# Attention scores in narrower pieces, a new order for the first 620 tasks, and a last projection by tiles

## The chip, the core and the metric

The kernel runs on one core of one Trainium2 chip. The metric is the time of one execution on the device in microseconds; each time below is from the chip. The engines are named as the profile names them: PE is TensorE's matmul, PEld its weight load, DVE VectorE, ACT ScalarE, POOL GpSimd, and SP the engine whose queue issues every DMA of this kernel.

## What is computed

Two layers follow each other. The first is attention over q, k and v of shape (4, 8, 768, 64), that is 4 batches, 8 heads, 768 positions of 64 numbers. A query sees two kinds of keys: its neighbours at a distance under 16, and one summary per block of 32 positions, whose key is the maximum over the block and whose value is the mean:

```python
k_sum = k.reshape(B, H, nb, block, D).max(axis=3)
v_sum = v.reshape(B, H, nb, block, D).mean(axis=3)
scores_l = scale * np.matmul(q, k.transpose(0, 1, 3, 2))
mask_l = np.abs(pos[:, None] - pos[None, :]) < window
scores_s = scale * np.einsum('bhsd,bhnd->bhsn', q, k_sum) + np.log(block)
scores_all = np.concatenate([np.where(mask_l, scores_l, -1e9), scores_s], axis=-1)
a = softmax(scores_all)
attn_out = np.matmul(a, np.concatenate([v, v_sum], axis=2))
```

The second layer takes the 3072 rows of 512 numbers, projects them to 2048, applies softplus and projects back: `out = softplus(x @ w_in) @ w_out`.

## The kernel before, in words

**Units of work.** The 768 queries of a batch are cut into chunks of 256; two chunks make a group, so there are six groups x = 0 to 5 of 512 rows. The attention of one chunk and one pair of head pairs (a head pair is two heads on the 64 + 64 partitions) is a block of tasks in `attention` (line 614): scores on PE, mask on DVE (line 657: adds the mask, takes the row minimum of the negated scores), exp on ACT (line 665), inverse on DVE, normalize on POOL, DVE or ACT (line 678 or 681), transposes of the probabilities (for group 0 by PE at line 698 and a copy by ACT at line 702; else by DVE at line 711 and a trip through DRAM), values on PE (line 744, for group 0 also 752), and copies of the result (line 765; 784 and 788 for a rounded high part by ACT and a low part by DVE).

**Scores.** A window is 64 queries with their 96 possible local keys; after those come 24 block summaries, 120 columns in all. In groups 2 to 5 the 120 columns are copied together and one matmul per window and head takes them all. In groups 0 and 1 ("apart") they lie apart: `scores` (line 629) first does the windows, 64 queries by 96 keys each (line 637), and then, per 128 queries and head, the 24 summaries in a second matmul (line 644). Each scores task of that kind covers two head pairs (`NG` = 2). The operands are plain fp32, and each such matmul stands as two records in the trace. There are eight such tasks. All scores share one PSUM tile, `sc`, which is free again when the mask has read it.

**Feed-forward.** `feed_forward` (line 1134) goes over 16 slices f of the hidden dimension. A product (line 1057, tile `ph`; in the later half line 1097, tiles `hx` and `hy`, by a scheme that saves one product in eight) is followed by softplus twice on ACT: "rounded" (line 1159, tile `gh`) and "exact" (line 1163). Their difference is the "rest" (line 1167, DVE, tile `gl`). Then `project` (line 1170) multiplies gh and gl with the two parts of w_out into four PSUM tiles `po`, one per 128 rows, accumulating over f. For f of the first and last slice there is a task per tile; between, all four tiles together. Each group goes through the slices in two halves, whose first result (`part`) is kept in DRAM. At the end, line 1197 reloads it, DVE adds it (line 1204), and the result is stored; for group 0, which comes last, one store per 128 rows (line 1225).

**Weights** arrive in pairs of slices, w0 to w7, and are split into a rounded part and a low part by a row of steps: magnitude (931 on DVE or 934 on ACT), clamp (938), shift (942), sign (946) on DVE, tail (952 on ACT or 955 on DVE), add_tail (960, POOL), high (964, ACT or DVE), low (971, DVE or POOL).

**What sets the order.** Every task has a number, in the order in which the program text declares it. `SEQUENCE` (line 147) lists all of them in the order in which they are issued; each engine works its own tasks in that order, and a task that waits holds back what is behind it on its engine. A letter behind a number picks another engine for a task: 54 is POOL's normalize, 54b ACT's. SP's queue is ordered by the same list.

Numbers that the text below uses: 3 to 22 are twenty warming matmuls on the identity (line 1249); 23, 25, 27, 29 load the keys of the first batch and 24, 26, 28, 30 take their maxima (line 352, DVE); 31 to 41, odd, load values whose sums PE forms in 32 to 42, even (line 430), and 43 is their mean (line 441, ACT); 44 and 47 load q of the first block, 82 and 85 that of the next head pairs, and 45 to 49 and 83 to 87 the value windows; 50, 66, 88, 104 are the scores of group 0 and 291, 316, 358, 383 those of group 1; 51, 67, 89, 105 the masks; 97 is the values task of chunk 0, second half of the heads; 120 to 123 ("keep", line 447) copy the first mean into its place; 125 and 134 load the two halves of the first slices of w_in, 161 the whole second pair; 218 is the first product of the feed-forward and 222 its rest.

Of the kernel before, what the change touches and what calls it, by code (L numbers as in the profile page):

```python
# [147 lines left out]
23 124 0 125 2 3 25 4 44 47 5 134 161 6 7 24 8 31 27 9 10 126 130 35 11 127 12 128 13 129 14 26 131 33 50 1 132 133a  # L148
51 15 16 52 17 85 18 135 136 66 19 137 20 138 29 21 22 45 82 162 139 37 163 166 53 32 164 54b 165 39 41 67 167 34 284
48 143 68 36 28 55 30 140 57 88 46 168 69 38 49 89 70 40 56 58 90 104 86 180 169 42 84 141a 105 142a 43 106 291 91 59  # L150
309 148a 92a 144 145 146 83 87 147 152 107 170 71 61 108 171 63 62 73 72 292 74 75 334 338 293 149 64 60a 181 93 182
95 183 316 77 79 184 94 96 97 351 76 80 150a 185 120 199 78 294 295a 153a 109 157 154 111 155 110 156 112 113 296 317
158 101 99 100 176 102 151a 159 218 336 115 117 160a 318 297 342 340 116 227 346 98a 118 186 285 121 335 219 339 228
172 173 174 220 319 358 221 229 222 230 223 376 289 337a 114 320b 234 235 224 175 344 286 204 231 177 298 301 299 290
321 241 343 236 287 300 242 187 237 178 341a 225 243 244 226 179 232 288 322 345 359 189 360 233 123 122 239 190 238
245 347 200a 188 302 310 361 383 201 362b 323 348 314 202 240 248 203 468b 472a 205 363 312 313 249 246 303 469b 467
384 326 324 191a 385 325 315 311 255 195a 206a 192 207 364 208 209 256 193 386 194 247 250 251 257 475 252 196 258 327
494b 259 387b 498a 262 349a 365 368 366 263 352 355 328 350 493 356 197a 269 388 367 198a 210a 270 476 353 357 354 495
253 264 211 389 65 643 265 212 214 213 254 271 266 501 272 215 273 369 519 477 260 377 380 216a 217 378 381 261 520a
478 526 521b 390 393 267 370 307 479a 305 308a 306a 372 392 391 382 480 268 373a 329 379 274 502 481 641 278 645 503  # L160
276 330a 332a 333a 277 275 529 394 547 331 548a 549 374a 375 395 399 482 485 484 470 279 397a 398 400 401 402 504 473
483 103 471 474 505 410 403 404 554a 281 282 405 644 506 411 406 412 413 530 507 407 649 647 408 414 409 531 557 486
659a 660b 417 532 533a 418 534 508 509 415 419 648 558 487a 420 510 511 496 500 658 653 304 497 416 421 499 559 655
535 422 642 650 646 665 651 652 424 560 425 561a 426 668 686 427 428 512 513 522 525 536 81 431 438 432 423 429 430
562 669 524 539 537 527 654 517 670 518a 489a 687 693a 523 528 538 563 439 433 440 434 435 441 442 688b 436 671 672b
696 715a 714 119 540 541a 491a 545 550 556 564 566 543a 492a 490a 673 697 719 716 567 552 565 445 446 447 448 437 443
449 656 553 551 555 698 444 396 371 674 450 544 722 741a 742a 699 700a 568 452 569 675 661 573 574 453 515 571a 280
572a 701 546a 516a 575 454 455 283 663 740 745a 576 451 577 578 456 458 488 723 457 459 678 676 657 460 461a 584 585
# [63 lines left out]
def kernel(  # L232
# [243 lines left out]
    class Places:  # L476


        def __init__(self, c, hp, sums, pads, apart):
# [11 lines left out]
            if apart:  # L491
                self.k_keys = [key for g in range(NG) for key in (sums.key_of(hp + g), (sums.k, hp + g))]
                self.keys = [[lambda g=g, s=s: sums.keys(hp + g)[:, s:s + KW] for s in starts] for g in range(NG)]
                self.k_sums = lambda g: sums.k()[:, hp + g]
            else:
                self.k_keys = [(k, "sums")]
                self.keys = [[lambda g=g, w=w: k()[:, g, w] for w in range(NWIN)] for g in range(NG)]
# [47 lines left out]
    class FirstPlaces:  # L545


        def __init__(self, hp, sums, own, sp):
# [29 lines left out]
            for i in range(n_c):  # L578
                w0 = i * NWIN
                tiles = SimpleNamespace(apart=True, q_keys=q_keys, v_keys=v_keys, k_keys=k_keys)  # L580
                tiles.q = lambda g, i=i: q(g)[:, i * CH:(i + 1) * CH]
                tiles.v = lambda g, w0=w0: v(g)[:, w0:w0 + NWIN]
                tiles.sums = lambda g: sums.first(hp + g)
                c0 = i * NG * NU * KS
                tiles.sp = lambda c0=c0: sp()[:, c0:c0 + NG * NU * KS].rearrange("p (u k) -> p u k", k=KS)
                tiles.sp_key = (sp, i)
                tiles.keys = [
                    [lambda g=g, s=s: sums.keys(hp + g)[:, s:s + KW] for s in starts[w0:w0 + NWIN]] for g in range(NG)
                ]
                tiles.k_sums = lambda g: sums.k()[:, hp + g]  # L590
                self.tiles.append(tiles)
# [22 lines left out]
    def attention(x, i, hp, tiles, by_pe):  # L614
# [518 lines left out]

    def feed_forward(x, f0, f1):
        po = [buffer([P, DM], F32, "po", "po", NT, psum) for _ in range(NT)]
        pairs = f0 > 0
        for f in range(f0, f1):
# [32 lines left out]
            def project(tokens, which, f=f, w2=w2, i2=i2, gh=gh, gl=gl):  # L1170
                for t in tokens:
                    for i, (a, part) in enumerate(((gh, 0), (gh, 1), (gl, 0))):
                        if (a is gl) in which:
                            nc.tensor.matmul(  # L1174
                                po[t](), lhsT=a()[:, t * P:(t + 1) * P], rhs=w2()[:, part, i2 * DM:(i2 + 1) * DM],
                                start=f == f0 and i == 0, stop=f == f1 - 1 and i == 2,
                            )
            parts = [(w2, i) for i in range(2)]
            if f in (f0, f1 - 1):
# [9 lines left out]
        order.group = f"e{x}.{f1}"  # L1189
        for i in range(0, NT, 2):  # L1190
# [28 lines left out]
            elif x == 0:  # L1219

                for t in range(2):
                    r0 = groups[x][0] * CH + (i + t) * P

                    def leave(t=t, r0=r0, ob=ob):
                        nc.sync.dma_start(out=out[r0:r0 + P, :], in_=ob()[:, t])
                    order.add(SP, 0, leave, [(ob, t)], [], size=256 * KiB, row=2048)
# [121 lines left out]
```

## Time and profile before

| | us |
|---|---|
| median of three runs | 616.25 |
| lowest and highest | 616.2 and 620.01 |
| the profiled execution | 617.61 |
| its span, first to last instruction | 615.8 |
| PE busy | 607.9 |
| DVE busy | 381.2 |
| ACT busy | 343.6 |
| POOL busy | 180.2 |

The profiled execution is one run by itself; its time is 1.8 us more than its span. Busy times come from the trace; matmuls are pipelined, so neighbouring records overlap.

### The profile page before, as it was taken

To read this page: it belongs to the slowest core of one execution; us is meant where nothing else is said; L and a number is where in the kernel's file an instruction comes from. 1 tells how busy PE (TensorE), PEld (TensorE's weight loads), DVE (VectorE), ACT (ScalarE), POOL (GpSimd) and SP (SyncE) were. 2 spreads that over 40 slices of the span, in tenths; PEclk is the share of its full clock that TensorE was granted. 3 is DMA by queue.
4 is the path that set the end of the run, shared out by engine and by line. 5 is a ranking of instruction groups with operands and counts; after the bars stand their busy time and mean duration, and the time that the engine had idled before them with its cause. 6 is when DMAs were issued, how large, how long until landed. Compare 5 with 4: busy or idle time off the path is not lost.

```text
span 615.8 us, 11948 instructions
## 1 busy us (share of the span) xinstructions
PE 607.9 (99%) x4444; PEld 509.2 (83%) x4444; DVE 381.2 (62%) x990; ACT 343.6 (56%) x846; POOL 180.2 (29%) x178
## 2 busy tenths in 40 slices
PE   8999999999999999999999999999999999999997
PEld 6577878888888888888888888889898989999996
DVE  4799997866565765533335679854765664554532
ACT  3889898977768675665356986432313222132211
POOL 4415334324115032210002563572410315012000
PEclk8999999999999999999999999999999999999999
DMA  8978679866868666666427620031040230020121
GB/s 303 304 253 256 213 244 281 265 218 200 277 203 259 203 214 205 209 205 212 134 69 237 238 74 1 1 141 64 2 171 2 102 137 1 35 103 1 40 98 68
DMA packets 66569, 96.12 MB, mean 156 GB/s; under 512 B 5872, under 2 KB 44624, under 8 KB 65744
## 3 DMA queue, kind: packets, MB, share of 16 engines
q1 hardware_dynamic: 66512, 95.36, 47.6%
q8 instruction: 35, 0.57, 0.4%
q14 instruction: 22, 0.18, 0.1%
HBM read 66.06 MB, written 27.26 MB: 152 GB/s over the span
## 4 chain that ended last, share of the span: by engine, by line
PE 88%; ACT 5%; DVE 2%; DMA 2%; issue 1%; POOL 1%; SPq 0%; ACTq 0%
PE po L1174 39%; PE ph L1057 21%; PE hx L1097 9%; PE hy L1097 7%; PE xo L744 4%; PE sc L637 4%; PE sc L644 1%; DMA first<-qT_dram 1%; DMA part<-ob 1%; PE vt L430 1%; PE warm L1249 1%; ACT t L934 1%; ACT L934 1%; ACT L1159 1%; ACT raw L952 1%
## 5 line engine op out<-in xcount | busy, mean ns | idle before, releaser
L1174 PE MATMUL po<-w,gh 128*128 128x512 f32 x768 | 202.8, 392 | 0.4 <-DVE w L971 0.4
L1174 PEld LDWEIGHTS po<-w,gh 128*128 128x128 f32 x768 | 141.3, 188 | 29.9 <-DVE w L971 0.8
L1057 PE MATMUL ph<-xw,w 128*128 128x512 f32 x672 | 161.5, 391 | 0.0
L1057 PEld LDWEIGHTS ph<-xw,w 128*128 128x128 f32 x672 | 125.2, 188 | 27.4 <-issue 0.5
L1174 PE MATMUL po<-w,gl 128*128 128x512 f32 x384 | 114.3, 392 | 0.0
L1174 PEld LDWEIGHTS po<-w,gl 128*128 128x128 f32 x384 | 70.9, 188 | 14.6 <-issue 0.3
L665 ACT ACTIVATE sp<-sp,nm 128x120 f32<-128x120 f32 x192 | 73.1, 383 | 7.1 <-DVE nm L657 6.9
L1159 ACT ACTIVATE gh<-hx 128x512 fp32r<-128x512 f32 x20 | 12.0, 599 | 107.6 <-DVE hx L1107 107.6
L960 POOL TENSOR_TENSOR t<-t,raw 128x1024 int32<-128x1024 int32 (+1 forms) x20 | 40.7, 2041 | 105.6 <-DVE t L946 70.7
L1167 DVE TENSOR_TENSOR gl<-ph,gh 128x512 fp32r<-128x512 f32 x56 | 38.2, 687 | 51.2 <-ACT ph L1163 51.0
L1159 ACT ACTIVATE gh<-ph 128x512 fp32r<-128x512 f32 x56 | 33.3, 597 | 37.6 <-PE ph L1057 37.3
L801 POOL TENSOR_TENSOR x<-r,x 128x512 fp32r<-128x512 f32 x23 | 30.6, 1339 | 67.9 <-DVE x L794 58.2
L657 DVE CUSTOM_DVE_ANT_0 sp<-sc,added 128x120 f32<-128x120 f32 x192 | 40.8, 278 | 8.6 <-PE sc L644 2.8
L665 ACT ACTIVATION_READ_ACCUMULATOR sp<-sp,nm 128x1 f32 x192 | 36.0, 188 | 0.0
L1097 PE MATMUL hx<-x,w 128*128 128x256 f32 x240 | 35.7, 285 | 0.0
L1097 PE MATMUL hx<-x,sw 128*128 128x256 f32 x240 | 35.5, 284 | 0.0
L1097 PEld LDWEIGHTS hx<-x,w 128*128 128x128 f32 x240 | 32.9, 190 | 2.1
L1097 PE MATMUL hy<-x,sw 128*128 128x256 f32 x240 | 34.4, 284 | 0.0
L1159 ACT ACT_TABLE_LOAD x23 | 29.5, 1283 | 6.3 <-PE ph L1057 5.9
L1163 ACT ACTIVATE ph<-ph 128x512 f32<-128x512 f32 x56 | 32.8, 590 | 0.0
L1097 PEld LDWEIGHTS hx<-x,sw 128*128 128x128 f32 x240 | 32.0, 190 | 0.8
L1097 PEld LDWEIGHTS hy<-x,sw 128*128 128x128 f32 x240 | 31.2, 192 | 0.2
(116 smaller groups left out, 821.8 us busy)
## 6 DMA issues: line engine op xcount, KB each, us to landing
squares<-tb SPq DMA_DIRECT2D x20, 512.0 KB
pT<-squares SPq DMA_DIRECT2D x80, 128.0 KB
raw<-w_out_dram SPq DMA_DIRECT2D x16, 512.0 KB
kf<-kT_dram SPq DMA_DIRECT2D x16, 384.0 KB
raw<-w_in_dram SPq DMA_DIRECT2D x6, 1024.0 KB
q<-qT_dram SPq DMA_DIRECT2D x20, 256.0 KB
raw<-r SPq DMA_DIRECT2D x20, 256.0 KB
part<-ob SPq DMA_DIRECT2D x10, 512.0 KB
```

The source lines that it names most:

```text
L637: nc.tensor.matmul(unit(g * NU + h * NPAIR + i)[r * QW:(r + 1) * QW, :KW if tiles.apart else KS], lhsT=q[rows, w * QW:(w + 1) * QW], rhs=t ...
L657: nc.vector.tensor_tensor_reduce(out=sp()[:, n], in0=unit(n), in1=added()[:, kinds.index((lows[w], lows[w + 1]))], scale=-SCALE, scalar=FL ...
L665: nc.scalar.activation(sp()[:, n], sp()[:, n], AF.Exp, bias=nm()[:, n:n + 1], scale=-1.0, accum_out=ss()[:, n:n + 1],)
L744: nc.tensor.matmul(xo()[h * D:(h + 1) * D, g * CH + w * QW:g * CH + (w + 1) * QW], lhsT=v[:, h * D:(h + 1) * D], rhs=queries(g, w, h)[:KW ...
L801: engine.tensor_tensor(to(1), a(), to(0).bitcast(F32), op=ALU.subtract)
L960: nc.gpsimd.tensor_tensor(a, a, word(0, I32), op=ALU.add)
L1057: nc.tensor.matmul(ph(), lhsT=lhs(part, cc), rhs=xw[cc][0]()[:, xw[cc][1], a], start=cc == 0 and n == 0, stop=cc == NCC - 1 and n == 2,)
L1097: nc.tensor.matmul(to()[:, half], lhsT=lhs(wa, cc), rhs=of_x(xa)[:, cc * CH:(cc + 1) * CH], start=cc == 0 and m == 0, stop=cc == NG - 1 an ...
L1159: nc.scalar.activation(gh(), all_of(), AF.Softplus)
L1163: nc.scalar.activation(all_of(), all_of(), AF.Softplus)
L1167: nc.vector.tensor_sub(out=gl(), in0=all_of(), in1=gh().bitcast(F32))
L1174: nc.tensor.matmul(po[t](), lhsT=a()[:, t * P:(t + 1) * P], rhs=w2()[:, part, i2 * DM:(i2 + 1) * DM], start=f == f0 and i == 0, stop=f == ...
```

## The change

It has three parts.

1. In `scores`, the apart kind handles the 24 summaries per window of 64 queries, right behind the window's own matmul and with the same queries as weights, where before it did them per 128 queries behind all windows. The lists `keys` now give pieces (first column, end column, key tile), and `k_sums` is gone.

```diff
-                            nc.tensor.matmul(
-                                unit(g * NU + h * NPAIR + i)[r * QW:(r + 1) * QW, :KW if tiles.apart else KS],
-                                lhsT=q[rows, w * QW:(w + 1) * QW], rhs=tiles.keys[g][w]()[rows], start=True, stop=True,
-                            )
-                for i in range(NPAIR if tiles.apart else 0):
-                    for h in range(2):
-                        rows = slice(h * D, (h + 1) * D)
-                        nc.tensor.matmul(
-                            unit(g * NU + h * NPAIR + i)[:, KW:KS],
-                            lhsT=q[rows, i * P:(i + 1) * P], rhs=tiles.k_sums(g)[rows], start=True, stop=True,
-                        )
+                            for k0, k1, k in tiles.keys[g][w]():
+                                nc.tensor.matmul(
+                                    unit(g * NU + h * NPAIR + i)[r * QW:(r + 1) * QW, k0:k1],
+                                    lhsT=q[rows, w * QW:(w + 1) * QW], rhs=k[rows], start=True, stop=True,
+                                )
```

2. The first 620 entries of `SEQUENCE` are put in another order. They hold the same tasks; the letter, and so the engine, of some fifty of them changes. Its beginning:

```diff
-23 124 0 125 2 3 25 4 44 47 5 134 161 6 7 24 8 31 27 9 10 126 130 35 11 127 12 128 13 129 14 26 131 33 50 1 132 133a
-51 15 16 52 17 85 18 135 136 66 19 137 20 138 29 21 22 45 82 162 139 37 163 166 53 32 164 54b 165 39 41 67 167 34 284
+44 0 47 3 23 4 25 2 5 125 161 6 31 27 7 33 85 8 9 10 11 24 12 13 14 26 15 50 82 130 126 127 128 29 16 129 17 134 18 51
+1 131 52 19 20 35 66 21 162 22 163 37 166 164 28 45 53 49 165 54b 32 34 48 67 167 39 68 55 30 132a 88 133 135 41 139a
...
```

Up to task 222, these change their engine: 132 and 139 (a high part and a tail, 512 wide) go from ACT to DVE; 133 and 142 (low parts, 512 wide) and 70 and 108 (normalize) from POOL to DVE; 60 (a copy of 512) and 150 (a high part) from DVE to ACT; 98 and 114 (copies) swap DVE and ACT. On SP, 120 and 121 move ahead of the value loads 86, 84 and 87.

3. The last two slices of the last group are projected tile by tile in a new function, `finish`: for each of the four tiles, the three matmuls of either slice, the addition, and the store. In the last tile, the first slice is added on its own; the second slice goes in halves of 256 columns to the PSUM tile of the scores, and each half is added and stored alone.

```diff
+        for t in range(NT - 1):
+            ob = (obs[t // 2], t % 2)
+            order.add(PE, 0.7, lambda t=t: p0([t], every), in0, [po[t]])
+            order.add(PE, 0.7, lambda t=t: p1([t], every), in1, [po[t]])
+            total(t, po[t], 0, DM, ob)
+            leave(t, 0, DM, ob)
+        t = NT - 1
+        whole = (obs[t // 2], t % 2)
+        order.add(PE, 0.7, lambda: p0([t], every), in0, [po[t]])
+        total(t, po[t], 0, DM, whole)
+        for k in range(2):
+            c0, c1, key = k * half, (k + 1) * half, (*whole, k)
...
+            order.add(PE, 0.36, lambda at=bank_of, c0=c0, c1=c1: p1([t], every, to=at, c0=c0, c1=c1), in1, [(other, k)])
+            total(t, (other, k), c0, c1, key, bank_of)
+            leave(t, c0, c1, key)
```

`total` is the addition of line 1204 over the given columns, `leave` the store of line 1225. The reloads stay where they were in the sequence.

## Rows read from the trace of the kernel before

**Rows 1.** The page: busy us, share of the span, instructions, per engine

```profile
PE 607.9 (99%) x4444; PEld 509.2 (83%) x4444; DVE 381.2 (62%) x990; ACT 343.6 (56%) x846; POOL 180.2 (29%) x178
```

**Rows 2.** Waits of PE: line <- whom, us in total, times, longest

```profile
PE warm L1249 <- POOL ident masks.py:199: 1.5, 1, 1.5
PE sc L637 <- PE vt L430: 0.9, 1, 0.9
PE sc L637 <- DMA first<-qT_dram: 0.7, 1, 0.7
PE xo L744 <- ACT pT L702: 0.6, 2, 0.3
PE po L1174 <- DVE w L971: 0.4, 1, 0.4
```

**Rows 3.** Timeline of PE: start, length (us), line, tile, shapes, count, [idle before]

```profile
1.46 7.07 PE L1249 MATMUL warm<-ident 128*128 128x256 f32 x24 [1.46 <-POOL ident masks.py:199]
9.25 0.56 PE L637 MATMUL sc<-kf,first 64*64 64x96 f32 x16 [0.72 <-DMA first<-qT_dram]
...
11.35 3.57 PE L1249 MATMUL warm<-ident 128*128 128x256 f32 x8
...
17.00 1.99 PE L1249 MATMUL warm<-ident 128*128 128x256 f32 x8
...
47.13 6.04 PE L1057 MATMUL ph<-xw,w 128*128 128x512 f32 x24
```

**Rows 4.** Windows: from:to, length, busy us of each engine, PE clock, DMA, GB/s

```profile
11.59:55.65 44.06, 42.50 (x534) 29.33 (x533) 38.84 (x153) 38.56 (x137) 15.98 (x10) 0.96 0.91 289
55.65:79.00 23.35, 23.35 (x170) 19.18 (x169) 22.93 (x59) 21.48 (x64) 8.82 (x6) 1.00 0.70 213
...
13.00:14.00 1.00, 1.00 (x4) 0.81 (x3) 0.97 (x6) 1.00 (x7) 0.00 (x0) 0.50 1.04 363
...
33.00:47.00 14.00, 13.41 (x232) 10.15 (x230) 12.55 (x38) 12.17 (x37) 3.76 (x3) 1.00 0.88 301
...
79.00:160.00 81.00, 81.00 (x736) 65.90 (x735) 59.83 (x198) 68.76 (x187) 29.95 (x35) 1.00 0.79 246
...
613.00:614.00 1.00, 0.00 (x0) 0.00 (x0) 0.00 (x0) 0.00 (x0) 0.00 (x0) 1.00 1.01 393
```

The busy times in a row of that view stand in the order PE, PEld, DVE, ACT, POOL.

**Rows 5.** Chain that ended last: start, us, what

```profile
31.86 0.49 PE sc L637 x16
32.34 0.56 PE sc L644 x8
...
41.61 1.08 PE xo L744 x32
...
80.73 0.98 PE sc L637 x32
```

**Rows 6.** Timeline of DVE: single steps on weights, a copy, a normalisation

```profile
26.48 1.22 DVE L971 TENSOR_TENSOR w<-t,w 128x1024 fp32r<-128x1024 f32 x1
27.61 0.42 DVE L964 CAST w<-t 128x512 fp32r<-128x512 f32 x1
...
38.02 0.68 DVE L765 COPY r<-xo 128x512 f32<-128x512 f32 x1
...
43.37 1.16 DVE L678 TENSOR_TENSOR sp<-sp,ss 128x960 f32<-128x960 f32 x1
```

**Rows 7.** Timeline of ACT: the first mean

```profile
29.88 0.59 ACT L441 ACTIVATE v<-vt 24x512 f32<-24x512 f32 x1 [1.51 <-PE vt L430]
```

**Rows 8.** Timeline of the end: a 256-wide DVE step, the last additions, matmul and stores

```profile
595.88 0.42 DVE L1107 TENSOR_TENSOR u<-hy,u 128x256 f32<-128x256 f32 x1
...
610.01 2.73 DVE L1204 TENSOR_TENSOR ob<-po,ob 128x512 f32<-128x512 f32 x4 [6.59 <-PE po L1174]
...
610.73 2.37 SPq L1225 DMA_DIRECT2D out_dram<-ob  x4
...
611.63 0.39 PE L1174 MATMUL po<-w,gl 128*128 128x512 f32 x1
```

More of the change, by code (lines that the diff above doesn't have):

```diff
@@ L153 @@
[L153 to L157, printed above, removed]
@@ L492, in __init__ @@
                 self.k_keys = [key for g in range(NG) for key in (sums.key_of(hp + g), (sums.k, hp + g))]
-                self.keys = [[lambda g=g, s=s: sums.keys(hp + g)[:, s:s + KW] for s in starts] for g in range(NG)]
-                self.k_sums = lambda g: sums.k()[:, hp + g]
+                self.keys = [
+                    [
+                        lambda g=g, s=s: [(0, KW, sums.keys(hp + g)[:, s:s + KW]), (KW, KS, sums.k()[:, hp + g])]
+                        for s in starts
+                    ]
+                    for g in range(NG)
+                ]
             else:
                 self.k_keys = [(k, "sums")]
-                self.keys = [[lambda g=g, w=w: k()[:, g, w] for w in range(NWIN)] for g in range(NG)]
+                self.keys = [[lambda g=g, w=w: [(0, KS, k()[:, g, w])] for w in range(NWIN)] for g in range(NG)]
             def load_q():
@@ L587, in __init__ @@
                 tiles.keys = [
-                    [lambda g=g, s=s: sums.keys(hp + g)[:, s:s + KW] for s in starts[w0:w0 + NWIN]] for g in range(NG)
+                    [
+                        lambda g=g, s=s: [(0, KW, sums.keys(hp + g)[:, s:s + KW]), (KW, KS, sums.k()[:, hp + g])]
+                        for s in starts[w0:w0 + NWIN]
+                    ]
+                    for g in range(NG)
                 ]
-                tiles.k_sums = lambda g: sums.k()[:, hp + g]
                 self.tiles.append(tiles)
@@ L1132, in hidden_pair, with finish, reload, total @@
         return [z, y]
+    def finish(x, po, final):
+        obs = [buffer([P, 2, DM], F32, "ob", "t", T_BUFS, dynamic=True) for _ in range(0, NT, 2)]
+        half = DM // 2
+        other = buffer([P, 2, DM], F32, "sc", "sc", 1, psum)
+        for i, ob in enumerate(obs):
+            def reload(i=i, ob=ob):
+                nc.sync.dma_start(out=ob(), in_=partial[x, 2 * i]())
+            order.add(
+                SP, 0, reload, [partial[x, 2 * i]], [(ob, 0), (ob, 1)], size=512 * KiB, row=2048, after=[products[-1]],
+            )
+        def total(t, src, c0, c1, key, at=None):
+            ob = obs[t // 2]
+            def read():
+                o = ob()[:, t % 2, c0:c1]
+                nc.vector.tensor_tensor(o, (at or src)()[:, c0:c1], o, op=ALU.add)
+            order.add(DVE, dve(c1 - c0), read, [src, (ob, t % 2)], [key])
+        def leave(t, c0, c1, key):
+            ob, r0 = obs[t // 2], groups[x][0] * CH + t * P
+            order.add(
+                SP, 0, lambda: nc.sync.dma_start(out=out[r0:r0 + P, c0:c1], in_=ob()[:, t % 2, c0:c1]), [key], [],
+                size=256 * KiB * (c1 - c0) // DM, row=4 * (c1 - c0),
+            )
+        (p0, in0), (p1, in1) = final
+        every = (False, True)
+        for t in range(NT - 1):
[10 more added lines that the diff above has]
+            c0, c1, key = k * half, (k + 1) * half, (*whole, k)
+            def bank_of(k=k):
+                return other()[:, k]
+            order.add(PE, 0.36, lambda at=bank_of, c0=c0, c1=c1: p1([t], every, to=at, c0=c0, c1=c1), in1, [(other, k)])
+            total(t, (other, k), c0, c1, key, bank_of)
+            leave(t, c0, c1, key)
     def feed_forward(x, f0, f1):
@@ L1136, in feed_forward @@
         pairs = f0 > 0
+        last, final = pairs and x == 0, []
         for f in range(f0, f1):
@@ L1189, in feed_forward @@
         order.group = f"e{x}.{f1}"
+        if last:
+            finish(x, po, final)
+            return
         for i in range(0, NT, 2):
@@ L1218, in feed_forward @@
                 )
[L1219 to L1226, printed above, removed]
             else:
```

45 lines of the change are left out of this document (27 added, 18 removed), and 6 rows, old and new, of the table SEQUENCE.

## The prediction

> **What bounds the kernel now.** I read the engines' busy shares first. TensorE (PE) is busy 607.9 of the 615.8 us span [rows 1], so only its own work or its few waits can give time back. Its waits are listed next [rows 2]: 1.5 us at the start, and 0.9, 0.7, 0.6 and 0.4 us after it. All but the last lie before 47.13 us, where the first projection of the feed-forward begins [rows 3]; the last is 0.4 us far behind. So from 47.13 us on, each microsecond of matmul taken away is one gained, provided that what feeds PE keeps up. Before that PE is busy too, but partly with filler: the 24 warming records from 1.46 us, and later ones. The next question is who stands right behind PE. The windows [rows 4] answer: VectorE (DVE) is busy 38.84 of 44.06 us from its first mask (11.59) to the end of its first rest of an activation (55.65), and 22.93 of 23.35 us from there to 79. It has 5.2 us of air in the first stretch and 0.4 in the second. That is the number on which I decide.
>
> **Part 1, sums in pieces of 64 queries.** Each fp32 matmul shows as two records. In one scores task of the "apart" kind, each of two head pairs now has 16 records of 64-wide weights and 96 columns (0.49 us) and 8 of 128-wide weights and 24 columns (0.56 us) [rows 5]: together 2.10 us. A record with wide weights takes 0.56/8 = 70 ns though it streams 24 columns; in the tasks that are not apart, 32 records of 64-wide weights and 120 columns take 0.98 us, 31 ns each. So the width of the weights and the change of shape cost, not the columns. The change makes 64 records per task: 32 of 96 columns, 32 of 24, all 64 wide.
> No row shows a 24-column record with 64-wide weights. From below: it hides altogether, the columns then add to the 120 of the other kind, and a task takes 0.98 us. From above: each added record takes 31 ns like its neighbours: 0.98 + 0.98 = 1.96 us. Between them stands the nearest row: the values, 32 records of 64-wide weights and 64 columns in 1.08 us [rows 5], which lie on two halves of the array, so 67 ns each per half. Scores lie on four quarters; 32/4 = 8 more per quarter at 67 ns add 0.54 us, and the shorter windows give back (120 - 96)/120 of 0.98, 0.20 us. I take 0.98 + 0.54 - 0.20 = 1.3 us, so 0.8 us less per task. There are eight such tasks (groups 0 and 1): 6.4 us of PE's time, six tasks before the first product and two behind it.
>
> **Part 2, the order of the first 620 positions.** The same tasks stay within these positions; their order changes, and the engine of some.
> The start: SP now issues both q blocks ahead of the keys, and the first weights behind both keys. Thirteen warming tasks stand ahead of the first scores where twelve stood. Before, twelve ended at 1.46 + 7.07 = 8.53 us and PE waited 0.72 for q until 9.25 [rows 3]; one more at 0.25 us a record (the 8 records of 17.00) ends at about 9.0, when q, first in the queue, has long landed. Scores end at 9.0 + 1.3 = 10.3. But in DVE's queue four steps on the first weights (2.0 us) stand before the first mask, and their load is now fifth; the fifth load of before, q, landed just before 9.25. So mask starts at about 9.1 + 2.0 = 11.1 us and not 11.59: 0.5 us earlier.
> DVE's list up to the first rest: it takes over from POOL two normalisations (1.16 each) and two low parts of 512 (half of the 1.22 of 1024), from ScalarE (ACT) a cast (0.42) and a tail (about the same): 4.4 us. It gives ACT one copy (0.68) and one cast (0.42): 1.1 us [rows 6]. A pair of copies is swapped at no cost. Net 3.3 us more. With the 0.5 us, DVE can finish the rest that ended at 55.65 by at most 5.2 - 3.3 + 0.5 = 2.4 us earlier, if it never waits. PE would offer more (6.4 us and the 2.2 us of waits after its start), so DVE sets the gain, and what is late next is the first rest. The four scores and the waits beyond that turn into idle PE before 55 us. From below the gain is that of the start alone, 0.5. I take 2.4, since the new order leaves DVE always something that is loaded; the two scores behind 47 us go into the same 2.4, as the list up to 79 us has only 0.4 us of air.
> SP also moves two small copies of the first mean (keep) ahead of three value loads. They wait for that mean, at 29.88 + 0.59 before [rows 7], and the loads behind them, 48 + 336 + 336 KiB, start only then. At 301 GB/s (33 to 47 us, [rows 4]) they take 2.5 us, so they are there around 34; their reader came at 41.61 [rows 5], some 2 to 3 us earlier now. The cost is nothing; without that cover it would be up to 2.5 us. The other moved loads lie within a queue that ran full, and I cost them at nothing.
> Between 79 and 160 us some 9 us more of work goes to DVE (sums of values, normalisations, casts), which is busy 59.83 of 81 us there [rows 4]: 21 us of air, so nothing.
>
> **Part 3, the last projection.** The matmuls are the same, only ordered by tile, with the last three in halves of 256. Now DVE starts its last 512-wide addition 0.43 us after the last matmul record's start (611.63) and ends at 612.74; four stores of 256 KiB, 335 ns apart in issue at least, run back to back [rows 8] until about 614.3 (393 GB/s from 613 to 614, [rows 4]); 615.8 ends the span. In the new order the last tile needs three additions after its first three matmuls: 0.68 + 0.34 + 0.42 us from 611.37, at 612.8, so 0.1 us later. But the stores before it are gone by then, and the last one has 128 KiB: 0.33 us instead of 0.67 at that rate, and no queue before it (some 0.1). Net 0.3 us gained; bounds 0 to 0.7.
>
> **Sum.** 2.4 + 0.3 = 2.7 us off the profiled execution's 617.61 us: 614.9. That execution was 1.36 above the median of the three runs, 616.25, so the forecast is 613.5.
>
> **Rivals.**
> (a) The small pieces are dear: 1.96 us a task. Then PE loses 8 x 0.14 = 1.1 us, PE and not DVE binds, with the tail 614.9. For it: 31 ns a record is the same at 96 and at 120 columns. Against: 70 ns with wide weights says that weights, not records, cost.
> The Trainium skill, TensorEngine Tiling (Array Packing), section Performance Considerations, gives each matmul about 60 cycles of overhead and warns against tiling a dimension that is small already, as 24 columns are. By that page the 32 added records cost an estimated 25 ns each, and a task 1.6 to 1.8 us; no run here shows such a record yet.
> (b) DVE is no bound, since PE needs few of its results: 6.4 + 2.2 + 0.3 off, 607.4. For it: 5.2 us of DVE's idle before. Against: 22.93 of 23.35 us busy right behind.
> (c) Slower: DVE, with 9 us more from 79 to 160 us, delivers rests late, and PE, which waited nowhere there, waits. It decides once more than 2.7 us of the 9 fall ahead of a rest that PE needs; with 6 us it is 619.5. Against it: 21 us of air.
> (d) The clock. The granted clock was 0.50, 1.2 of 2.4 GHz, at 13 to 14 us [rows 4], after PE had idled 0.72 us and run small scores; 8 warming records took 3.57 us in place of 1.99 [rows 3]. More idle PE from 17 to 45 us could bring that again; two such stretches of 1.6 us each, half hidden, give some 615.3.
>
> **Chances.** Forecast 0.60 (its own range 612.0 to 615.0), (a) 0.15, (b) 0.06, (c) 0.12, (d) 0.07. The range from 610.0 to 617.5 leaves out (b), most of (c) and the edges. A measurement of this kernel tells about 1%, 6.2 us, from no change. Faster by more needs (b) or DVE's bound being soft: 0.09. Slower by more needs nearly all 9 us of (c): 0.02. Within 1%: 0.89.
>
> **What would show it.** Right: a scores task of groups 0 and 1 near 1.3 us, no record of 128-wide weights in it; first scores near 9.0; DVE over 95% busy from 11 to 55 us and the first product near 45; PE with 4 us or more of new idle before 55; no wait of PE from 80 to 160; last store issued near 613.1. Wrong: a task near 2 us (a), PE without idle before 47 and the end 8 us earlier (b), waits for gl from 80 us on (c), a clock of 0.50 after 17 us (d).

## The result, and the profile after

The changed kernel takes 620.15 us (median of 20 runs, 618.08 to 621.85) beside 616.74 us for the kernel before in the same session: ratio 1.0053, with a 95% interval of 1.0041 to 1.0064. So it is some 3.3 us slower. I had forecast 613.5 us, and at most 617.5. The profiled execution took 620.38 us, its span is 618.6 us, 2.8 more than before.

The page of the kernel after, busy times (columns as in [rows 1]):

```profile
PE 605.3 (98%) x4575; PEld 507.6 (82%) x4575; DVE 393.0 (64%) x1014; ACT 338.5 (55%) x834; POOL 165.0 (27%) x161
```

PE's busy time fell by 2.6 us, and yet the span grew by 2.8: PE stands idle for 5.4 us more (618.6 - 605.3 = 13.3 us, where it was 615.8 - 607.9 = 7.9). DVE does 11.8 us more work, POOL 15.2 us less. The waits of PE in the kernel after, which answer to [rows 2] (line, whom it waited for, us in total, times, longest):

```profile
PE xo L746 <- ACT pT L704: 3.9, 4, 2.2
PE warm L1298 <- POOL ident masks.py:199: 1.4, 1, 1.4
PE sc L646 <- DVE ss L674: 1.1, 1, 1.1
PE xo L746 <- DVE gl L1217: 1.1, 2, 0.7
PE sc L646 <- issue: 1.0, 1, 1.0
PE sc L1224 <- DVE ob L1153: 1.0, 1, 1.0
PE po L1224 <- DVE gl L1217: 0.6, 1, 0.6
```

They sum to 10.1 us where those of [rows 2] sum to 4.1. The longest is that of the last values ahead of the feed-forward. PE's timeline of the kernel after, just there:

```profile
43.97 1.59 PE L746 MATMUL xo<-pT,first 96*64 96x64 f32 x32 [2.19 <-ACT pT L704]
45.49 1.97 PE L754 MATMUL xo<-pT,v 24*64 24x256 f32 x8
47.40 5.78 PE L1059 MATMUL ph<-xw,w 128*128 128x512 f32 x16
```

In the profile before, the values started at 45.01, so beside it the new kernel is still 1.04 us ahead; the first product, at 47.13 in [rows 3], is 0.27 us late. But that execution of the kernel before was an unusual one. Its granted clock was 0.50 from 12 to 15 us, where eight warming records took 3.57 us [rows 3, 4], and its mean clock is 0.997; of 118 executions of this kernel timed beside the experiments, 104 show 0.999 or 1.0. The run e3 below has the same scores and the same order up to the last projection, and its clock stays at 1.00 there. PE in e3, the same eight warming records and the values:

```profile
11.28 1.99 PE L1296 MATMUL warm<-ident 128*128 128x256 f32 x8
43.49 1.17 PE L744 MATMUL xo<-pT,first 96*64 96x64 f32 x32 [0.29 <-ACT pT L702]
```

Its first product starts at 45.60. Against e3 the new kernel is 0.48 us late at the values and 1.80 us late at the first product. Between the two lies the clock. Windows of PE in the kernel after (from:to, length, busy us, granted clock, DMA share, GB/s):

```profile
42.00:44.00 2.00, 0.03 (x2) 1.00 1.02 429
45.00:51.00 6.00, 6.00 (x29) 0.50 0.88 270
```

PE idles for nearly all of 42 to 44 us, and behind that the granted clock is 0.50 (1.2 of 2.4 GHz) for 6 us; before, it was 1.00 from 44 to 52. With 0.76 from 44 to 45 and 0.83 from 51 to 52 the full-speed time lost is 0.24 + 3.0 + 0.17 = 3.4 us. The window of the first scores task in the kernel after shows 64 records in 1.31 us, as forecast (it counts the instructions on the tile `sc` alone: busy us of PE, PEld and DVE, then clock, DMA share and GB/s):

```profile
9.93:11.24 1.31, 1.31 (x64) 1.27 (x64) 0.00 (x0) 1.00 0.99 351
```

Last, how full DVE is, from its first mask to the values (from:to, length, DVE busy, clock, DMA share, GB/s); the kernel before:

```profile
11.59:45.01 33.42, 28.48 (x121) 0.95 0.91 284
```

e3, the same work at full clock:

```profile
11.52:43.49 31.97, 28.47 (x121) 1.00 0.94 297
```

and the kernel after:

```profile
11.72:43.97 32.25, 31.23 (x126) 1.00 0.97 309
```

DVE's idle time there fell from 4.94 us to 1.02, as I wanted, but its work rose by 2.75 us. And only 3.50 us of idle time are there to be filled at full clock; the other 1.4 belong to the low clock of the execution that I had read.

### The profile page after: what moved, and what is told of

The parts are those of the page before. It is cut to its first block, busy times and chain, and to the rows that moved or that the text cites. A ratio compares the mean times of both kernels' runs of the same rounds, so it can differ in the third digit from the quotient of the medians.

```text
span 618.6 us, 12198 instructions
## 1 busy us (share of the span) xinstructions
PE 605.3 (98%) x4575; PEld 507.6 (82%) x4575; DVE 393.0 (64%) x1014; ACT 338.5 (55%) x834; POOL 165.0 (27%) x161
## 4 chain that ended last, share of the span: by engine, by line
PE 86%; DVE 7%; ACT 3%; DMA 3%; SPq 1%; issue 1%; DVEq 0%; ACTq 0%
PE po L1224 40%; PE ph L1059 22%; PE hx L1099 9%; PE hy L1099 7%; PE xo L746 3%; PE sc L646 2%; DVE sp L659 2%; ACT sp L667 1%; DMA raw<-w_in_dram 1%; DMA squares<-tb 1%; DVE t L948 1%; DVE tb L713 1%; DVE gl L1217 0%; PE xo L754 0%; DVE t L940 0%
## 5 line engine op out<-in xcount | busy, mean ns | idle before, releaser
L1059 PEld LDWEIGHTS ph<-xw,w 128*128 128x128 f32 x672 | 126.9, 190 | 28.0 <-issue 1.2
```

What stands on the lines that cost most here:

```text
L1059: nc.tensor.matmul(ph(), lhsT=lhs(part, cc), rhs=xw[cc][0]()[:, xw[cc][1], a], start=cc == 0 and n == 0, stop=cc == NCC - 1 and n == 2,)
```

## The experiments

Each kernel was timed beside the kernel before; ratios are to it, with 95% intervals. Line numbers are those of each run's own kernel.

**The parts alone.** Four kernels, each the kernel before with some of the three parts of the diff:

```diff
e1_scores_only         + part 1
e2_order_only          + part 2
e3_tail_only           + part 3
e4_scores_and_order    + part 1, + part 2
```

> The kernel before with the scores' part alone: the sums in pieces of 64 queries, the old order and the old last projection. Theory (the new order is what loses): each of the eight scores tasks in the order of before is 0.8 us shorter; those ahead of 47 us are in part given to waits for DVE, the three at 39 to 69 us are kept, so 2 to 5 us faster than before, first product of ph at 45 to 47 us. Rival A (the pieces are what loses, later in the kernel): no faster than before, with waits of PE for DVE's weight steps that before does not have. Rival B (the tail loses): 2 to 5 us faster too, so this run does not tell the theory from it.

> The kernel before with the new order of the first 620 positions alone: old scores of 2.10 us, old last projection. Theory (the new order loses): slower than before by 3 to 7 us: PE idles about 1 to 2 us ahead of the values behind the last transposes, the granted clock falls to 0.50 for some us behind it, and waits for gl between 80 and 160 us come back in part. Rival A (the pieces lose): within 1 us of before or faster. Rival B (the tail loses): within 1 us of before or faster.

> The kernel before with the new last projection alone: tile by tile, the last tile in halves. Theory (the tail is a small loss): the second half's products wait about 1 us for DVE's addition of the first half, which the profile of the changed kernel shows, so the span is 0.3 to 1 us longer than before. Rival B (the tail loses the 3.4 us): 3 us longer or more. My forecast was 0.3 us shorter.

> The changed kernel with the old last projection: pieces of 64 queries and the new order. Theory: the changed kernel less the tail's 0.3 to 1 us, so 2.4 to 3.1 us slower than before, with the wait of 2.2 us ahead of 44 us and the granted clock of 0.50 behind it. Rival B (the tail loses): 1 us or more faster than before.

Measured: e1 614.24 us, 0.9951 (0.9936 to 0.9967), faster by more than its interval; e2 620.66 us, 1.0073 (1.0049 to 1.0097); e3 617.57 us, 1.0009 (0.9996 to 1.0022), not told from no change; e4 618.77 us, 1.0037 (1.0017 to 1.0056). So the pieces gain what I had expected from all parts together, and the order loses it and more, whichever scores stand in it. The tail is small.

Why the pieces gain in the old order is seen in DVE's waits. Those of the kernel before, from 11 to 50 us (same columns as the waits of PE):

```profile
DVE sp L657 <- PE sc L644: 2.8, 2, 1.9
DVE sp L657 <- POOL w L971: 2.2, 1, 2.2
DVE xw L788 <- ACT xw L784: 1.1, 1, 1.1
DVE ss L672 <- ACT sp L665: 0.4, 1, 0.4
```

The 2.2 us lie ahead of the first mask. Of the rest, 2.8 us are DVE waiting for PE's scores, in two waits of 1.95 and 0.89 us; in e3, at full clock, the same two take 0.50 and 0.89. Shorter scores take these away without any new order: e1 has neither. DVE in e1, to the values, and PE's timeline there:

```profile
10.78:40.21 29.43, 28.02 (x120) 1.00 1.05 330
```

```profile
40.21 1.17 PE L746 MATMUL xo<-pT,first 96*64 96x64 f32 x32 [0.44 <-ACT pT L704]
...
42.32 2.12 PE L1059 MATMUL ph<-xw,w 128*128 128x512 f32 x8
```

The values start 4.80 us earlier than in the profile before, and 3.28 us earlier than in e3, which is the like comparison: the first mask is 0.74 earlier, DVE idles 1.41 us for 3.50, and its work is 0.45 less (0.74 + 2.09 + 0.45). The times of e3 and e1, 617.57 and 614.24, are as far apart. In e2, with the old scores, the same view reads

```profile
11.71:44.60 32.89, 31.31 (x125) 1.00 0.96 307
```

DVE is just as full as after, with some 31.3 us of work, and the shorter scores move the values by only 0.63 us (44.60 to 43.97). Between e1 and the kernel after the values' start differs by 3.76 us; in DVE's time that is 3.21 of work and 0.94 of a later mask, less 0.39 of idle time. This sum says what DVE did until then, not that the values needed all of it: their last wait in the kernel after is for ACT, and in e6 below they start at 41.16 us in the new order, with 28.46 us of DVE's work ahead of them.

**Is it the idle stretch and its clock, or ACT's order?** Two kernels on e4 as base. The first fills the idle stretch, the second removes its cause.

```diff
         def values():
+            if (x, i, hp) == (0, 1, 2):
+                for _ in range(5):
+                    nc.tensor.matmul(
+                        xo()[:, :2 * P].rearrange("p (o c) -> p o c", o=2), lhsT=ident(),
+                        rhs=ident().rearrange("p (o c) -> p o c", o=1).broadcast_to([P, 2, P]), start=True, stop=True,
+                    )
```

> Scores' pieces and new order with the old last projection (618.8 us in its own run), and ahead of the values that wait 2.2 us for ACT's copy, five products of the identity into the output tile that these values overwrite: about 2.2 us of TensorE work in the idle stretch, that nobody reads. Nothing else moves. Theory (the idle of 2.2 us at 41.4 to 43.6 us brings the granted clock of 0.50 behind it, and this costs about 3 us): the values start as before, at 43.6 to 44.1 us, the granted clock stays at 1.00 from 44 to 52 us, the first product of ph starts near 46 us, and the time is 615 to 616.5 us. Rival (the clock falls for another reason, or its fall costs nothing because DVE is what is waited for): a clock of 0.50 in 44 to 52 us all the same, or a clock of 1.00 and no gain; 618 to 619.5 us either way.

```diff
-78 185 150 109 295a 184 153a 111 157 110 154 316 155 156 112 101
+78 109 295a 184 111 110 112 185 150 153a 157 154 316 155 156 101
```

> Scores' pieces and new order with the old last projection, but ACT's two copies of pT (0.55 us each) ahead of its four weight steps (a tail of 1.19 us, a cast, a magnitude, another tail) where the new order has them behind. Theory (these four steps are what the values wait for): the values start at about 42 us for 43.6, the idle ahead of them is under 0.6 us, the granted clock stays at 1.00, first product of ph near 44.5 us; 614.5 to 616 us. Rival (the copies only wait for something else, or what the steps feed is late in its turn): values at 43 us or later, or the first product at 47 us behind a wait for the weights; 617.5 us or more.

e5: 619.95 us, 1.0034 (1.0018 to 1.0050), no better than e4. The windows of PE show that the filler did its work:

```profile
42.00:44.00 2.00, 2.00 (x10) 1.00 0.98 413
44.00:48.00 4.00, 4.00 (x50) 1.00 0.73 220
48.00:52.00 4.00, 4.00 (x18) 1.00 1.04 320
```

The clock stays at 1.00 and the first product starts at 46.26 for 47.41 in e4, but later PE waits longer for the rest `gl`. Its timeline in e5:

```profile
81.09 1.15 PE L752 MATMUL xo<-pT,v 120*64 120x64 f32 x32 [1.24 <-DVE gl L1175]
...
218.38 1.15 PE L752 MATMUL xo<-pT,v 120*64 120x64 f32 x32 [2.14 <-DMA pT<-squares]
```

The wait of 1.24 us was 0.71 in the kernel after, and that of 2.14 us, for a transfer, stands in none of the lists of PE's waits of before, after, e1 to e4, e6 and e10. So the idle stretch does bring the lower clock, and yet in this order it does not set the time: my theory fell. All ten runs of e5, at mean clocks of 0.996 to 1.0, still take 618.3 to 621.1 us. The kernel after says the same with its own 20 runs: the six at a mean clock of 0.996 to 0.999 took 618.47 to 619.96 us, the fourteen at 0.992 to 0.994 took 618.08 to 621.85, their medians are 1.3 us apart, and even the six lie above the 616.74 of before.

Where the time goes in e5 is seen from the first product to the end. Windows of PE there in e1, e5 and e6, the next run (from:to, length, busy us, clock, DMA share, GB/s):

```profile
42.32:612.20 569.88, 563.84 (x3946) 1.00 0.46 145
46.26:618.90 572.64, 564.05 (x3946) 1.00 0.45 144
43.26:617.20 573.94, 564.54 (x3946) 1.00 0.45 145
```

PE has the same work in all three, but behind the first product it idles 6.0 us in e1, 8.6 in e5 and 9.4 in e6. What an earlier product or a better clock gives, the new order loses again in waits behind it; which of its steps these come from is not shown.

e6: 619.5 us, 1.0045 (1.0020 to 1.0069). The copies were the cause of the idle stretch, for the values start at 41.16 us without a wait, but the next thing is late. PE's timeline of e6:

```profile
43.26 2.11 PE L1059 MATMUL ph<-xw,w 128*128 128x512 f32 x8
47.75 1.43 PE L1059 MATMUL ph<-xw,w 128*128 128x512 f32 x5 [2.39 <-POOL w L973]
```

Products that start 4.15 us earlier wait 2.39 us for their weights: the four weight steps of ACT that I had put back were needed too.

**The tail.** Two variants of e3, one with the halves in two tiles, one without halves.

```diff
-        other = buffer([P, 2, DM], F32, "sc", "sc", 1, psum)
+        other = [buffer([P, 2, DM], F32, "sc", "sc", 1, psum), bank([P, DM], "other")]
```

> The kernel before with the new last projection, the second half of the last tile in a tile of its own where the changed kernel has both halves in two banks of one tile. Theory (the wait of 1.0 us of the second half's products for the addition of the first is between two users of one tile): no such wait, last addition 0.7 us earlier behind the last product than in the run of the tail alone, about 0.7 us faster than that run (617.57), so 616.5 to 617. Rival (the products wait for something else of DVE, its additions in order): the wait stays, 617.5 us.

```diff
-        for t in range(NT - 1):
+        for t in range(NT):
...
-        t = NT - 1
...
-            leave(t, c0, c1, key)
```

> The kernel before with the last projection tile by tile, the last tile whole as the other three (no halves, no addition in between). Theory (the halves are what the new tail pays for): one addition of 0.69 us behind the last product as before, the stores spread over 1.36 us each: 0.5 to 1 us faster than the tail alone (617.57), within 0.5 us of the kernel before. Rival (working tile by tile itself is the loss): 617.5 us.

e7: 616.85 us, 0.9994 (0.9979 to 1.0009). e8: 617.65 us, 1.0011 (0.9987 to 1.0036). All three tails are within what can be told from no change, so only the traces speak. The end of the kernel after, DVE and then PE:

```profile
612.76 1.37 DVE L1153 TENSOR_TENSOR ob<-po,ob 128x512 f32<-128x512 f32 x2 [0.67 <-PE po L1224]
614.24 0.42 DVE L1153 TENSOR_TENSOR ob<-sc,ob 128x256 f32<-128x256 f32 x1
615.38 0.42 DVE L1153 TENSOR_TENSOR ob<-sc,ob 128x256 f32<-128x256 f32 x1 [0.71 <-PE sc L1224]
```

```profile
613.02 0.39 PE L1224 MATMUL po<-w,gl 128*128 128x512 f32 x1
613.24 0.40 PE L1224 MATMUL sc<-w,gh 128*128 128x256 f32 x2
...
614.72 0.50 PE L1224 MATMUL sc<-w,gh 128*128 128x256 f32 x2 [0.96 <-DVE ob L1153]
```

The second half's matmuls, which write another bank of the same tile, wait until DVE has read the first half. In e7 they go on at once, and the last two additions follow each other:

```profile
612.77 0.42 DVE L1151 TENSOR_TENSOR ob<-sc,ob 128x256 f32<-128x256 f32 x1
613.12 0.42 DVE L1151 TENSOR_TENSOR ob<-other,ob 128x256 f32<-128x256 f32 x1
```

From the last matmul into `po` (613.02 after, 611.55 in e7) to the end of the last addition it takes 2.78 us after and 1.99 in e7. The wait belongs to the shared tile.

**Which stretch of the order, and whose engines?**

```diff
e9_new_then_old
-296 317 158 113 98 351 102 151a 159 160a 218
+296 317 158 113 351 100 176 102 151a 159 218
e10_old_then_new
-156 112 113 296 317 158 101 99 100 176 102
+156 112 113 121 101 99 296 317 158 98 102
e11_old_engines
-30 132a 88 133 135 41 139a
+30 132 88 133a 135 41 139
```

(e9 is set against e4, e10 against e1, each followed by all that is left in the other order; e11 sets 53 letters back.)

> Scores' pieces, the old last projection, and the new order only up to the values of the fourth attention step (position 173 of 620, about 44 us), then the old order of all that is left. Theory as it stands after the filler and the copies (the first stretch of the new order puts PE 3.4 us later at these values than the pieces in the old order do, and the stretch behind it then keeps DVE too full to win any of it back): values at 43 to 44 us, no waits for gl at 81 and 92 us, 616 to 618 us. Rival (only the first stretch loses): 618.8 us, as with the whole new order. Rival (only the stretch behind it loses): 614 to 615.5 us, as with the pieces in the old order.

> The other way round: scores' pieces, old last projection, the old order up to the same values (position 168 there), then the new order of all that is left. Theory: values at 40.2 us and the granted clock at 1.00 behind them, as with the pieces in the old order, then new waits of PE of 2 to 3 us in all for gl and w between 45 and 160 us, since DVE has more to do there: 616 to 618 us. Rival (only the first stretch loses): 614.2 us. Rival (only the stretch behind it loses): 618.8 us.

> Scores' pieces, old last projection, the new order, but each of the first 620 steps on the engine that it had before: about 12 us of work back from DVE, 17 us more on POOL. Theory (DVE's load is what the new order is late by): fewer waits for gl between 80 and 160 us, 1 to 3 us faster than the new order with its own engines (618.77). Rival (the order of the steps, not their engines, is what loses): 618.5 us or more, POOL's steps of 2.0 us for 1.16 being late in their turn.

e9: 619.09 us, 1.0033 (1.0014 to 1.0051). e10: 615.91 us, 0.9979 (0.9969 to 0.9989). e11: 632.8 us, 1.0253 (1.0232 to 1.0275). The first stretch, up to 44 us, alone brings nearly the whole loss (e9); the stretch behind it alone costs 615.91 - 614.24 = 1.7 us (e10), so the two do not simply add up. Most of the 1.7 us stands in waits for `gl`; these are PE's in e10, where e1 has 0.6 us of each:

```profile
PE xo L751 <- DVE gl L1174: 1.6, 2, 1.3
...
PE po L1181 <- DVE gl L1174: 0.8, 2, 0.6
```

e11 refutes the simple form of DVE's load: with the old engines the new order is some 13 us slower still by the ratios (1.0253 beside e4's 1.0037). Its order is made for its engines.

**Repairs of the new order.** On e4, with `296 317` behind `288`; with six letters back; and with `296 317` and e6's swap together.

```diff
e13_next_step_later
-112 101 99 296 317 158 113 98 351 102 151a 159 160a 218 336 115 117 186 285 288 318
+112 101 99 158 113 98 351 102 151a 159 160a 218 336 115 117 186 285 288 296 317 318
e14_first_engines_back
-132a 133 139a 70a 108a 142
+132 133a 139 70 108 142a
e15_both_repairs
-78 185 150 109 295a 184 153a 111 157 110 154 316 155 156 112 101 99 296 317 158
+78 109 295a 184 111 110 112 185 150 153a 157 154 316 155 156 101 99 158
```

> Scores' pieces, new order, old last projection, with two of DVE's steps of the next attention step moved back: the transpose (1.24 us) and the mask (some 1.8 us) of the second half's first steps, which the new order has ahead of the last low parts of the first product's operands and the old order behind them. Theory (DVE is full from 11 to 48 us in the new order, and these two stand ahead of what the first products wait for): values still at 43.6 us, but the first half's products done 2 to 3 us earlier (the third group of them at 49.5 to 50.5 us for 52.7), 615.5 to 617 us. Rival (the values' wait for ACT and the clock behind it set the time, not DVE): 618.3 us or more.

> Scores' pieces, new order, old last projection, with six steps of the stretch up to 44 us back on the engines that they had before (a high part and a tail on ACT, two low parts and two normalizations on POOL): 4.8 us less on DVE, 1.3 us more on ACT, 6.6 us more on POOL. Theory (DVE's load in this stretch): values at 41 to 42 us, 616 to 617.5 us. Rival (POOL's normalizations of 2.0 us for 1.16 stand between scores and transposes, and its low parts of 1.3 us for 0.7 ahead of the sums): values at 44 us or later, 619 us or more.

> The run with DVE's two steps moved back, and ACT's two copies of pT ahead of its four weight steps as in the run of the copies. Theory (each repair alone leaves the other's wait as the last one): values near 41.5 us, no wait of 2.4 us for w at 47.75 us, granted clock 1.00, 614 to 615.5 us. Rival: 617.5 us or more, with the wait for w still there or with waits for gl at 81 and 92 us that take all of it back.

None repairs it: e13 620.3 us, 1.0058 (1.0041 to 1.0075); e14 619.73 us, 1.0042 (1.0030 to 1.0054); e15 619.58 us, 1.0040 (1.0027 to 1.0053). My text on e13 was also wrong in one thing: the old order too has these two steps ahead of the low part `102`, so they are no difference between the orders. In e14 the rival held: PE waits 1.42 us at 32.46 us for ACT, and the values start at 46.20. In e15 a wait for w of 1.9 us remains (its profiled execution, at 622.51 us, is the slowest of its six).

**The six steps in the good order.** Here nothing but letters changes, on e1 as base.

```diff
e16_old_order_new_engines
-132 133a 139 70 108 142a
+132a 133 139a 70a 108a 142
e17_two_normalizations
-70 108
+70a 108a
e18_four_weight_steps
-132 133a 139 142a
+132a 133 139a 142
```

> Scores' pieces in the old order, with the six steps on the engines of the new order: 4.8 us more on DVE in the stretch to 42 us, where it is busy for 95% and more in the run of the pieces alone (614.24). Theory (DVE's time ahead of the first product is what counts): first product 2 to 4 us later than 42.3 us, 616 to 618 us. Rival (the steps are shorter on DVE and stand on the chain from scores to values, so that they pay for themselves): first product at 41.5 to 42.5 us, 613.5 to 614.5 us.

> Pieces of 64 queries in the old order, with two normalizations of the stretch up to 42 us on DVE (1.16 us each) where the old order has them on POOL (2.0 us): 2.3 of the 4.8 us that the run with all six moved. Theory (DVE's load counts, whichever step it is): first product 1.5 to 2.3 us later than 42.3 us, 615.7 to 617 us beside 614.2 for the pieces alone. Rival (a normalization stands on the chain from scores to values and is shorter on DVE, so that these two pay for themselves): within 0.7 us of 614.2.

> The other four of the six: a high part and a tail of the weights from ACT, two low parts of the weights from POOL, to DVE (0.43, 0.69, 0.69 and 0.69 us). Theory (DVE's load): first product 1.5 to 2.5 us later than 42.3 us, 615.7 to 617 us, and with the run of the two normalizations the 4.5 us of all six. Rival (only these four cost, or only the normalizations): all of the 4.5 us here (618 to 619 us), or none (within 0.7 us of 614.2).

e16: 618.69 us, 1.0034 (1.0020 to 1.0047), as slow as e4; by the ratios that is (1.0034 - 0.9951) x 617 = 5.1 us more than e1. Its DVE to the values:

```profile
11.16:43.74 32.58, 31.51 (x124) 1.00 0.98 317
```

Against e1 the values are 3.53 us later: 3.49 us of more work, 0.38 of a later mask, less 0.34 of idle time. The clock is at 1.00 there, and the span of this execution is 3.9 us longer than e1's (616.1 for 612.2). In other executions the clock takes its share: the six at a mean clock of 0.996 to 1.0 took 617.37 to 618.62 us, the six at 0.988 to 0.994 took 618.75 to 621.91. So some 4 of the 5 us come without it. Six letters suffice to lose what the pieces gained.

e17: 617.86 us, 1.0004 (0.9992 to 1.0016), and e18: 615.81 us, 0.9960 (0.9940 to 0.9980): by the ratios 3.3 and 0.6 us more than e1. The 0.6 us lie within the intervals of e1 and e18, so the four weight steps alone are not told from nothing, as the rival in the text on e18 had it; and the two together give 3.9 of the 5.1 us. In e18 the values come 1.24 us later, for 1.04 us of more work of DVE (29.06 us).

In e17 the loss has a second source. PE's timeline, and its window behind that:

```profile
28.19 0.42 PE L651 MATMUL sc<-kf,q 64*64 64x96 f32 x8 [1.78 <-issue]
```

```profile
30.00:36.00 6.00, 6.00 (x60) 0.50 0.92 255
```

A wait of 1.78 us (0.89 in e1), then 6 us at a clock of 0.50. The values are 3.39 us late, some 3 us of it by the low clock. The times say the same: the one run of e17 with a mean clock of 0.999 took 615.59 us, the ten at 0.992 to 0.997 took 617.18 to 618.82.

**The best found.** e1's pieces with e7's tail:

```diff
e12_scores_two_banks   + part 1, + part 3 with the last half in a tile of its own
```

> The pieces of 64 queries in the old order, with the new last projection whose last half has a tile of its own. Both parts were measured alone: 0.9951 and 0.9994 of the kernel before; if they add, 0.9945, some 613.8 us beside a kernel before of 617. If the stores collide in the changed tail, 0.9951 or more.

e12: 614.33 us, 0.9961 (0.9949 to 0.9973), the same as e1 within the intervals. The pieces alone, at 0.9951, are the version to keep.

## Why the prediction was wrong

- **Part 1's price was right.** "I take 1.3 us": 1.31 measured. Rival (a), 1.96 us, is out. The Trainium skill, TensorEngine Tiling (Array Packing), section Performance Considerations, states some 60 cycles of overhead for each matmul, and I had estimated 1.6 to 1.8 us a task from it; this trace does not bear that out for 64-wide pieces on four quarters (1.31 us, 20 ns a record).
- **The step that failed** is in part 2: "so DVE sets the gain", with the 5.2 us of DVE's air booked as something that the new order fills, and the first rest up to 2.4 us earlier. That air was mostly DVE waiting for PE's scores (2.8 us) and, through ACT, for PE's values; 1.4 us of it came from the low clock of the one execution that I read, which I used for rival (d) and not here. Part 1 alone took 2.1 us of it away at full clock (e1 beside e3), and the first product came at 42.32 us in the old order; I had given part 1 no gain of its own. The first rest itself, DVE's timeline of the kernel after and then of e1:

```profile
54.79 0.69 DVE L1217 TENSOR_TENSOR gl<-ph,gh 128x512 fp32r<-128x512 f32 x1 [1.14 <-ACT ph L1213]
```

```profile
50.74 0.64 DVE L1169 TENSOR_TENSOR gl<-ph,gh 128x512 fp32r<-128x512 f32 x1
```

It ended at 55.65 before, at 55.48 after, and at 51.38 in e1; after, DVE stands idle for 1.14 us ahead of it and waits for ACT, so there it was not DVE's work that set it. I listed DVE's busy shares and not what DVE waited for; one more view of the trace before would have shown it.
- **The 3.3 us of moved steps** were counted about rightly (2.75 us more work of DVE to the values), but set against air that part 1 takes away by itself. On a DVE that the pieces have already filled they are a loss: in e16, 3.5 us at the values and some 5 us of time. The larger part comes with the two normalizations (e17), whose late values are mostly the clock's; the four weight steps cost little alone (e18).
- **Where I said "first product near 45".** It came at 47.40. ACT's four weight steps ahead of its last copy held PE for 2.19 us, and the clock went to 0.50. This is rival (d), with 3.4 us lost in one stretch for my 3.2 in two. e5 shows that in this order the clock is not what binds; e17 shows that elsewhere it costs some 3 us.
- **Part 2 behind 79 us.** "21 us of air, so nothing" was wrong: waits for `gl` of 0.71, 0.37 and 0.58 us stand at 82, 94 and 159 us, and e10 prices the new order behind 44 us at 1.7 us. They are not all the new order's: e1, which reaches this part earlier in the old order, has two such waits of 0.6 us. Rival (c) has the right mechanism, with less weight than its 6 us. An average share of 74% busy did not exclude it.
- **The start.** First scores at 9.93 us for 9.0: the 26 warming records took 8.63 us (7.33 to 8.30 us in e2, e4, e6, e9 and e13 to e15, which begin alike). They last 634 ns each until 6.6 us and mostly 379 ns behind that, where before the shorter ones begin at about 4.6 us; the granted clock reads 1.00 throughout, so no row here gives the cause. Mask at 11.72 for 11.1: the weights whose four steps stand ahead of it were there at 9.7 us and not at 9.1. So the 0.5 us of the start, the term that I took for the lower bound, was not gained: the first mask is 0.13 us later than before.
- **Part 3** was forecast at -0.3 us. I had the three additions in sequence but not that the second half's matmuls wait 0.96 us for the first addition, so the last addition ends some 0.9 us later than I thought (at 615.80, where 1.44 us of additions from 613.45 would end at 614.89), and the smaller last store gives back 0.3 (span end 2.8 us behind it for 3.1). The interval of e3, 0.9996 to 1.0022, holds both signs.
- **"No wait of PE from 80 to 160", "last store near 613.1"** were to show me right and showed me wrong; "4 us or more of new idle" (3.7 by 55 us) and "DVE over 95% busy" (97% to the values, 94% to 55 us) came nearly true, and meant the opposite of a gain.

That the new order with its engines loses what the pieces gain is shown (e1, e4, e16). What stays open: why no single repair brings the new order to e1's time, and which steps cause the waits that take back e5's better clock. That both orders are made for their own choice of engines (e11, e14) is what the runs show; a rule for a good pair they do not give.

## What to carry to other kernels

Before booking an engine's idle time as room for more work, look at what ended each idle stretch: if it was the engine you are about to make faster, the room goes with it. Test the parts of a change singly, since a gain in one (0.9951) and a loss in another (1.0073) stood in one number here. See whether the execution that you read is a usual one: here 1.4 us of the idle time belonged to it alone. An order and its choice of engines belong together; 4.8 us of steps moved onto an engine that is 95% full in one stretch put the end of that stretch off by 3.5 us, though it is busy for only 62% of the run.

## What the runs showed of the hardware

Some short waits of PE were followed by a granted clock of 0.50, the lower of its two levels (1.2 of 2.4 GHz): 2.19 us idle, then 6 us at 0.50 (after); 1.78 us idle, then 6 us at 0.50 (e17); a wait of 0.75 us that ends at 44.60 us, with the clock still at 1.00 behind it, and then 3 us at 0.50 (e2). PE's windows in e2:

```profile
45.00:46.00 1.00, 1.00 (x30) 1.00 0.63 217
47.00:50.00 3.00, 3.00 (x8) 0.50 0.89 279
```

Yet the wait of 2.39 us in e6, within 44 to 48 us, was followed by none. PE's windows in e6:

```profile
44.00:48.00 4.00, 1.61 (x7) 1.00 1.03 311
48.00:52.00 4.00, 3.84 (x16) 1.00 0.99 308
```

So the length of a wait alone did not tell whether the clock would fall. That a wait was the cause is shown for the first one only, since in e5, with products in its place, the clock stayed at 1.00. Four executions that issue the same work up to 12 us point the same way: PE waited 0.72 us (before) and 1.04 us (e8) for q ahead of the first scores, and the clock stood at 0.50 from 12 to 15 and from 12 to 14 us; it waited 0.36 us (e7) or not at all (e3), and the clock stayed at 1.00.

In the scores, 64 records of 64-wide weights took 1.31 us, where 48 records, 16 of them with 128-wide weights, took 2.10 [rows 5]: more pieces of one width were cheaper than fewer of two.

Two halves of a product in different banks of one tile were held apart by 0.96 us, and in two tiles by nothing. That wait goes with the tile; no run tells whether the program or the chip sets it.
